# Gated mix of two linear-attention blocks: the load of B's wo moved behind the scratch round trip of M_A

## The chip, the cores and the metric

The kernel runs on one core of a Trainium2 chip. Times are device microseconds of one execution. The engines are PE (TensorE, matmuls; its weight loads are listed apart as PEld), DVE (VectorE), ACT (ScalarE), POOL (GpSimd) and SP (SyncE, which here only issues DMAs).

## The reference

Two linear-attention blocks A and B with their own weights read the same input x (2048 rows of 640, bf16; 32 heads of 20). Their outputs are mixed by a gate per row.

```python
def _A_ref(x, wqkv, wo):          # _B_ref is the same
    q, k, v = ...                 # (x @ wqkv), split into 32 heads of 20
    phi = lambda t: jnp.where(t > 0, t + 1, jnp.exp(t)) + 1e-6
    pq, pk = phi(q), phi(k)
    kv = jnp.einsum("bhsd,bhse->bhde", pk, v)
    z = jnp.einsum("bhsd->bhd", pk)
    num = jnp.einsum("bhqd,bhde->bhqe", pq, kv)
    den = jnp.einsum("bhqd,bhd->bhq", pq, z)[..., None] + 1e-6
    o = num / den
    return (heads of o side by side) @ wo

g = sigmoid((x * gate_w).sum(-1, keepdims=True))
return g * a + (1 - g) * b
```

## The kernel before

The kernel never forms v. It computes G = xᵀ·phi(k) (640 by 640), from it KV of each head by a product with wv and a mask, and M = KV·wo, one 640 by 640 matrix for each block. With the gate and the denominators folded into the scaled queries pqA and pqB, the output is pqA·M_A + pqB·M_B. Most large products are done by a Strassen-like scheme (sums of blocks on DVE, seven products in place of eight on PE, the products added up in PSUM).

The order of the work is written out by hand: within a `manual_schedule` block each engine runs its instructions in the order of the program, and waits on semaphores where it needs another's result. DMAs are issued by SP in program order too (the loads of the start and two of the last stores also by ACT). An instruction of SP that waits holds all that stand behind it.

The part around the change is the end of the third part, from the last k chunks of B to the first products of the output:

- `g_pass(1, DT - 1, 0, ...)` (L897; matmuls L424) makes the fifth block of rows of G of B in two runs of matmuls. Between the runs, and after it, six calls of `m_block` (L868) make M_A: each multiplies a masked block of 120 rows of KV of A (40 rows in the last) with `woA`, the wo of A (PE L872), and ACT copies the result into `M[0]` (the tile `MA`; the sixth into a tile `m`) at L877. SP then stores these rows into `m_rows`, a scratch tensor in DRAM (L878).
- `z_rows` (L510, PE L516) sums phi(k) of B over the rows, between the fourth and the fifth `m_block`.
- A DMA (L903) then reads all of `m_rows` back into `M[0]`. The rows come back in another order: row 5p + m goes to partition p, place m. It waits for all six stores to land.
- `p_diff` and `g_strassen(1, ...)` (L906; matmuls L453) follow: the other four fifths of G of B in seven products. Around the products, DVE does: `rec_pass` (L573, the reciprocals of the denominators), `k_sum(1, 4)`, then TM0, the difference of the two halves of M_A (L495, done by the helper at L592), which is the first reader of the reloaded `M[0]`; then `scale` (L642), five multiplications of pqB by R, the spread reciprocals, which ACT copies out of PSUM at L634; with two additions (L470, L508) that finish blocks of G. The addition of L470 reads a PSUM tile that a later product of PE adds to.
- After the stage, `kvt_mm` (L542, PE) and `kvt_mask` (L549, DVE) make KV of B, `p1` (L653) the first product of the output with `M[0]`, and `m_unit` and `m_half` (L567, PE) make M_B from KV of B and `woB`, the wo of B: the first readers of `woB`. From there to the end PE runs the products of the output (L653), DVE their additions (L658) and the sums of operands (L592), and SP stores the output (L673).

`load_wo(1, nc.sync)` (L735) loads `woB`, 800 KB, with one DMA issued by SP (L741). Its tile is the buffer of `woA` (one buffer in the pool `wpool` under the tag "wo"), so its DMA waits until the last matmul of the six `m_block`s has read `woA`. In the program it stands at L895, in front of the six stores of L878.

Of the kernel before, what the change touches and what calls it, by code (L numbers as in the profile page):

```python
# [32 lines left out]
def kernel(  # L33
# [11 lines left out]
    nc = tc.nc  # L45
# [12 lines left out]
    def new_stage(name):  # L58

        if stage:  # L60
            stage.pop().close()
        if name is not None:
            held = ctx.enter_context(ExitStack())
            stage.append(held)
            pools["ps"] = held.enter_context(late_pool(name))
# [373 lines left out]
    def k_sum(b, k):  # L439

        b11, b12 = [pk[:, 0:hc, n * HF:(n + 1) * HF] for n in range(2)]
        b21, b22 = [pk[:, hc:ST, n * HF:(n + 1) * HF] for n in range(2)]
        t = TK[b]
        left, right = {1: lambda: (b12, b11), 2: lambda: (b22, t[1]), 3: lambda: (b22, b12), 4: lambda: (b21, t[2])}[k]()
        add_rows(t[k], left, right, ALU.subtract)
# [148 lines left out]
    def p_diff(rows):  # L594

        up = slice(SH + rows.start, SH + rows.stop)
        add_rows(D3[:, :, rows], pqT[0][:, :, rows], pqT[0][:, :, up], ALU.subtract)
# [137 lines left out]
    def load_wo(b, eng):  # L735
        wo_sb[b] = wpool.tile([P, NG, D], BF16, tag="wo", name=f"wo{'AB'[b]}")
        if b == 0:
            eng.dma_start(out=wo_sb[0][:K6, 0:DT], in_=wo_dram[0][0:DT * K6].rearrange("(j p) f -> p j f", p=K6))
            eng.dma_start(out=wo_sb[0][:D - DT * K6, DT], in_=wo_dram[0][DT * K6:D])
            return  # L740
        eng.dma_start(out=wo_sb[b][:KG], in_=wo_dram[b].rearrange("(j p) f -> p j f", p=KG))  # L741
# [46 lines left out]
    with tc.manual_schedule():  # L788
# [79 lines left out]
        def m_block(g, slot):  # L868
            n = blocks[g][1]
            pt = ps("mA", slot)  # L870
            for hf in range(2):
                nc.tensor.matmul(  # L872
                    pt[:n, hf, 0:HF], lhsT=kv6[:n, g * K6:g * K6 + n], rhs=wo_sb[0][:n, g, hf * HF:(hf + 1) * HF],
                    start=True, stop=True,
                )
            to = M[0][:n, g, :] if g < DT else work.tile([P, D], BF16, tag="osb", name="m5", bufs=3)[:n]
            nc.scalar.copy(out=to.rearrange("p (b n) -> p b n", b=2), in_=pt[:n, :, 0:HF])  # L877
            nc.sync.dma_start(out=m_rows[g * K6:g * K6 + n, :], in_=to)  # L878
# [13 lines left out]
        TK[1][1] = t1[:]  # L892
        for k in (1, 2, 3):
            k_sum(1, k)
        load_wo(1, nc.sync)  # L895
        new_stage("after")
        g_pass(1, DT - 1, 0, lambda: [m_block(g, 2 + g) for g in (0, 1)])  # L897
        m_block(2, 2)
# [2 lines left out]
        m_block(4, 2)  # L901
        m_block(5, 3)
        nc.sync.dma_start(out=M[0][:], in_=m_rows[:].rearrange("(p m) d -> p m d", m=DT))  # L903
        part = [slice(n * RB, (n + 1) * RB) for n in range(4)]
        p_diff(part[0])
        g_strassen(1, lambda: z_pass(1, zr, 1), 3, 1)  # L906
# [105 lines left out]
```

## Time and profile before

| | us |
|---|---|
| median of 3 runs | 192.91 |
| lowest, highest run | 192.71, 193.56 |
| the profiled execution | 193.14 |
| its span | 191.4 |
| PE busy | 183.9 |
| DVE busy | 155.9 |
| ACT busy | 86.6 |
| POOL busy | 8.6 |

The profile is of one execution. Its span runs from the first to the last thing that it records; the execution's time holds a little more around it. A timeline row gives the start and the length in us, the engine and line, the operation with output and inputs, shapes, and how many instructions are merged; in brackets stands the idle time of the engine before it, and what ended it. "DMA to landing" is the time from the issue of a DMA by an engine to its last bytes. PE's ends are modelled: a row of matmuls that follow each other overlaps a little with the next, so starts are compared with starts. The granted clock of PE was 0.999 of full speed.

### The profile page before, as it was taken

The numbers are of one execution on the slowest core, as the hardware profiler recorded it, in microseconds if no ns is written. First come the engines' busy times: TensorE is split into PE (matmuls) and PEld (weight loads), VectorE is DVE, ScalarE is ACT, GpSimd is POOL, SyncE is SP. The second block draws the span as 40 slices with busy tenths as digits, with TensorE's granted clock in tenths as the row PEclk, the third lists the DMA queues.
The fourth block names the chain that finished last, engine by engine and source line by source line (L and its number), as shares of the span: only waits on it lengthen the run. The fifth ranks groups of instructions, "written<-read, shape, count | busy, mean of one in ns | idle before, by whom it ended". The sixth has DMA issues, their size and how long they took to land.

```text
span 191.4 us, 3678 instructions
## 1 busy us (share of the span) xinstructions
PE 183.9 (96%) x1485; PEld 123.7 (65%) x1494; DVE 155.9 (81%) x267; ACT 86.6 (45%) x134; POOL 8.6 (5%) x23
## 2 busy tenths in 40 slices
PE   8999999999999999999999999999968999999992
PEld 3666657765577677676666656766746776777771
DVE  1478868998998999997989878999397989788553
ACT  2055497555851622547786858642511611121110
POOL 8900000000000000000000000000000000000000
PEclk9999999999999999999999999999999999999999
DMA  6976449990050000005000000047400002312112
GB/s 192 305 146 69 99 82 323 328 251 32 2 171 3 0 0 0 3 0 171 0 3 2 0 0 3 0 122 224 171 0 3 0 3 87 118 41 103 69 69 70
DMA packets 19759, 15.64 MB, mean 82 GB/s; under 512 B 9502, under 2 KB 19614, under 8 KB 19742
## 3 DMA queue, kind: packets, MB, share of 16 engines
q1 hardware_dynamic: 18878, 14.59, 27.9%
q10 hardware_dynamic: 864, 0.82, 1.3%
q8 instruction: 11, 0.18, 0.4%
q14 instruction: 6, 0.05, 0.1%
HBM read 10.00 MB, written 3.44 MB: 70 GB/s over the span
## 4 chain that ended last, share of the span: by engine, by line
PE 84%; DVE 7%; DMA 5%; issue 1%; SPq 1%; ACT 1%; DVEq 0%; ACTq 0%
PE kA L250 12%; PE qA L294 11%; PE kB L250 11%; PE gs L453 9%; PE q L348 7%; PE ox L653 5%; PE oy L653 5%; PE oz L653 5%; DVE pqTB L642 3%; DMA m_rows<-m 3%; PE ow L653 2%; PE gB L424 2%; PE gA L424 2%; DMA MA<-m_rows 2%; PE warm L186 2%
## 5 line engine op out<-in xcount | busy, mean ns | idle before, releaser
L250 PEld LDWEIGHTS <-xT 128*128 128x128 bf16 x320 | 31.4, 99 | 15.0 <-issue 0.3
L230 DVE TENSOR_SCALAR e<-e 128x640 bf16<-128x640 bf16 (+2 forms) x56 | 19.3, 345 | 6.9 <-ACT e L225 6.7
L250 PE MATMUL kB<-wkB,xT 128*128 128x320 bf16 x160 | 24.2, 299 | 0.0
L250 PE MATMUL kA<-wkA,xT 128*128 128x320 bf16 x160 | 23.4, 306 | 0.0
L294 PE MATMUL qA<-xT,wqA 128*128 128x512 bf16 x96 | 22.2, 379 | 0.2
L294 PEld LDWEIGHTS <-wqA 128*128 128x128 bf16 x100 | 11.6, 118 | 9.3 <-issue 0.3
L225 ACT ACTIVATE e<-kA 128x640 bf16<-128x640 f32 x16 | 11.1, 704 | 12.4 <-PE kA L250 12.3
L453 PEld LDWEIGHTS <-xn 128*128 128x128 bf16 x128 | 12.2, 98 | 5.2 <-issue 0.5
L225 ACT ACTIVATE e<-kB 128x640 bf16<-128x640 f32 x16 | 11.3, 708 | 9.0 <-PE kB L250 8.9
L239 DVE SCALAR_TENSOR_TENSOR pk<-kA,e 128x640 bf16<-128x640 f32 x16 | 13.2, 825 | 1.7
L239 DVE SCALAR_TENSOR_TENSOR pk<-kB,e 128x640 bf16<-128x640 f32 x16 | 13.2, 824 | 1.5
L225 ACT ACTIVATE e<-qA 128x1024 bf16<-128x1024 f32 x10 | 10.2, 1023 | 8.6 <-PE qA L294 8.1
L697 ACT COPY u<-ox 128x320 f32<-128x320 f32 x8 | 3.4, 425 | 21.9 <-PE ox L653 21.9
L225 ACT ACTIVATE e<-q 128x512 bf16<-128x512 f32 x18 | 10.8, 597 | 5.4 <-PE q L348 3.8
L653 PEld LDWEIGHTS <-xT 128*128 128x128 bf16 x85 | 8.0, 98 | 3.1 <-DVE xT L592 0.2
L653 PEld LDWEIGHTS <-pqTA 128*128 128x128 bf16 x85 | 7.9, 98 | 2.9 <-issue 0.2
L653 PEld LDWEIGHTS <-pqTB 128*128 128x128 bf16 x80 | 7.8, 98 | 3.0
L453 PE MATMUL gs<-pk,xn 128*128 128x320 bf16 x64 | 9.5, 299 | 0.0
L348 PE MATMUL q<-xT,wqB 128*128 128x512 bf16 x32 | 9.5, 379 | 0.0
L658 DVE TENSOR_TENSOR osb<-oz,u 128x320 bf16<-128x320 f32 (+1 forms) x18 | 8.0, 452 | 1.6 <-PE oz L653 0.9
L681 ACT COPY p1s<-ox 128x320 f32<-128x320 f32 x8 | 3.4, 426 | 12.8 <-PE ox L653 12.8
L424 PEld LDWEIGHTS <-xn 128*128 128x128 bf16 x64 | 6.3, 98 | 3.0 <-issue 0.4
(145 smaller groups left out, 318.8 us busy)
## 6 DMA issues: line engine op xcount, KB each, us to landing
out_dram<-osb SPq DMA_DIRECT2D x14, 160.0 KB, 1.8
xn<-in_A_x_dram SPq DMA_DIRECT2D x3, 640.0 KB, 6.1
wqA<-in_A_wqkv_dram SPq DMA_DIRECT2D x1, 800.0 KB
wvA<-in_A_wqkv_dram SPq DMA_DIRECT2D x1, 800.0 KB, 9.3
wkB<-in_B_wqkv_dram SPq DMA_DIRECT2D x1, 800.0 KB, 6.1
wqB<-in_B_wqkv_dram SPq DMA_DIRECT2D x1, 800.0 KB
wvB<-in_B_wqkv_dram SPq DMA_DIRECT2D x1, 800.0 KB, 4.7
woB<-in_B_wo_dram SPq DMA_DIRECT2D x1, 800.0 KB, 6.3
```

The costliest lines, as they stand in the source:

```text
L186: nc.tensor.matmul(warm[:, 0, :], lhsT=one_l, rhs=one_r, start=True, stop=True)
L225: nc.scalar.activation(out=to, in_=part, func=ACT.Exp)
L230: nc.vector.tensor_scalar(self.e, self.e, 1.0, EPS, op0=ALU.min, op1=ALU.add)
L239: nc.vector.scalar_tensor_tensor(out=dst, in0=src, scalar=1.0 + EPS, in1=e, op0=ALU.add, op1=ALU.max)
L250: nc.tensor.matmul(pt[:, hf, 0:HF], lhsT=xT[:, c, i * P:(i + 1) * P], rhs=wk[b][:, c, hf * HF:(hf + 1) * HF], start=(c == 0), stop=(c == D ...
L294: nc.tensor.matmul(dst, lhsT=mixed(wq[b][:, c, :], m), rhs=xT[:, c, n * HB:(n + 1) * HB], start=first, stop=last,)
L348: nc.tensor.matmul(dst, lhsT=left(c), rhs=right(c), start=first and k == 0, stop=k == len(cs) - 1, skip_group_check=not first,)
L424: nc.tensor.matmul(pt[:, hf, 0:HF], lhsT=xn[:, i, c * P:(c + 1) * P], rhs=pk[:, i, hf * HF:(hf + 1) * HF], start=(i == 0), stop=(i == ST - 1),
L453: nc.tensor.matmul(pt[:, n, 0:HF], lhsT=left[:, i, n * P:(n + 1) * P], rhs=right[:, i, :], start=(first and i == 0), stop=(i == hc - 1), s ...
L642: nc.vector.tensor_tensor(out=pqT[b][:, m, :], in0=pqT[b][:, m, :], in1=rec, op=ALU.mult)
L653: nc.tensor.matmul(dst, lhsT=left[:, c, r0:r0 + P], rhs=right[:, c, :], start=(first and c == 0), stop=(c == DT - 1), skip_group_check=not ...
L658: nc.vector.tensor_tensor(out=dst, in0=acc, in1=sb, op=ALU.add)
```

## The change

The one call moves from its place in front of the stage "after" to a place behind the reload of `M[0]`. Everything else is the same text. After the change SP meets, in this order: six stores into `m_rows`, the reload of `M[0]` from it, the load of `woB`, the stores of the output.

```diff
         for k in (1, 2, 3):
             k_sum(1, k)
-        load_wo(1, nc.sync)
         new_stage("after")
         g_pass(1, DT - 1, 0, lambda: [m_block(g, 2 + g) for g in (0, 1)])
         m_block(2, 2)
@@ -901,6 +900,7 @@
         m_block(4, 2)
         m_block(5, 3)
         nc.sync.dma_start(out=M[0][:], in_=m_rows[:].rearrange("(p m) d -> p m d", m=DT))
+        load_wo(1, nc.sync)
         part = [slice(n * RB, (n + 1) * RB) for n in range(4)]
         p_diff(part[0])
         g_strassen(1, lambda: z_pass(1, zr, 1), 3, 1)
```

## The prediction

> **What bounds the kernel now.** The page first: its head, the busy times, and the shares of the chain that ended last.
>
> ```profile
> span 191.4 us, 3678 instructions
> PE 183.9 (96%) x1485; PEld 123.7 (65%) x1494; DVE 155.9 (81%) x267; ACT 86.6 (45%) x134; POOL 8.6 (5%) x23
> ...
> PE 84%; DVE 7%; DMA 5%; issue 1%; SPq 1%; ACT 1%; DVEq 0%; ACTq 0%
> ```
>
> PE is the bound: 191.4 - 183.9 = 7.5 us of the span is not PE's. But 7% of the chain is DVE and 5% DMA, so somewhere PE is held by them. The list of waits says where; columns are total us, times and longest:
>
> ```profile
> DVE TM L592 <- DMA MA<-m_rows: 3.3, 1, 3.3
> ...
> PE gs L453 <- DVE GT L470: 1.8, 1, 1.8
> ...
> PE mid L542 <- DVE KVT L549: 0.8, 1, 0.8
> ```
>
> These are one story. DVE idles 3.3 us for the reloaded M_A, and PE then waits twice (1.8 and 0.8) for DVE. A wait of SP's queue says why the reload was late (same columns), and the timeline of SP gives the times (start, us):
>
> ```profile
> SPq L741 <- PE mA L872: 39.4, 1, 39.4
> ```
>
> ```profile
> 125.17 0.34 SPq L741 DMA_DIRECT2D woB<-in_B_wo_dram  x1
> 125.61 2.71 SPq L878 DMA_DIRECT2D m_rows<-MA  x5
> 128.41 0.34 SPq L878 DMA_DIRECT2D m_rows<-m  x1
> ```
>
> SP issues in order. The load of wo of B (woB) takes woA's buffer, so it waits for the last matmul that reads woA; the six stores stand behind it and leave only from 125.61, although ACT had the first rows ready far earlier:
>
> ```profile
> 120.19 1.29 ACT L877 CAST MA<-mA 120x640 bf16<-120x640 f32 x2 [0.71 <-PE mA L872]
> ...
> 123.28 1.31 ACT L877 CAST MA<-mA 120x640 bf16<-120x640 f32 x2
> 124.80 0.69 ACT L877 CAST MA<-mA 120x640 bf16<-120x640 f32 x1 [0.21 <-PE mA L872]
> 125.39 0.68 ACT L877 CAST m<-mA 40x640 bf16<-40x640 f32 x1
> ```
>
> The landings, from the DMA issues of the page, from the view of line 878 and from the chain in order of time:
>
> ```profile
> woB<-in_B_wo_dram SPq DMA_DIRECT2D x1, 800.0 KB, 6.3
> ```
>
> ```profile
> DMA to landing us min/median/max: 5.7/5.9/6.1
> ```
>
> ```profile
> 128.41 5.13 DMA m_rows<-m
> 133.54 0.02 issue
> 133.56 4.29 DMA MA<-m_rows
> ```
>
> woB lands at 125.17 + 6.3 = 131.5. The first store, out at 125.61, took 5.7 us or more, so it landed not before 131.3; the last one at 133.54. The stores queue behind woB's bytes as well as behind its issue. The reload then lands at 133.56 + 4.29 = 137.85.
>
> **The change part by part.** Nothing is added or removed: one DMA issue of 0.34 us on SP moves behind six stores and one reload. The planned instruction order of PE, DVE, ACT and POOL stays as it was. There are four steps.
>
> (1) Stores. Freed of woB they leave behind their ACT copies: the first near 120.19 + 0.65 = 120.8, the fourth at 123.28 + 1.31 = 124.6, the fifth at 124.80 + 0.69 = 125.5, the last at 125.39 + 0.68 = 126.1 (126.2 with the issue of the fifth before it, 2.71 / 5 = 0.54 each). The last store thus leaves 128.41 - 126.2 = 2.2 us earlier.
>
> (2) Their landing. No row shows a store into the scratch with nothing ahead of it. The nearest are the stores of the output, also from 128 or fewer partitions into DRAM; the page's row and the spread over all 18 of them:
>
> ```profile
> out_dram<-osb SPq DMA_DIRECT2D x14, 160.0 KB, 1.8
> ```
>
> ```profile
> DMA to landing us min/median/max: 1.6/1.8/2.4
> ```
>
> Lower bound 1.6, upper bound 5.13 (the same store behind woB). I take 1.9, near the lower one: same direction, size and queue. Landing 128.1, against 133.54: 5.4 us earlier, of which 2.2 from the issue and 3.2 from the emptier queue.
>
> (3) The reload, issued at 128.1, with woB issued 0.4 us behind it. Alone it took 4.29, which gives 132.4. Worst, the two share the engines evenly and both end when both are done: woB and the 800 KB of stores together took 133.54 - 125.17 = 8.4 us, so 128.1 + 8.4 = 136.5. I take 132.4, since the stores behind woB landed after it, not beside it: a transfer of this queue waits for those ahead. The Trainium skill, "DMA: Bandwidth & Descriptors", section "Queues, rings and completion order", says that each DMA engine consumes descriptors in ring order but without a barrier between them; by the first half the reload keeps its 4.29, by the second it could lose some of it, and the landings here speak for the first half.
>
> (4) DVE and PE. DVE's timeline, with ACT's one row that matters:
>
> ```profile
> 133.88 1.94 ACT L634 CAST R<-exB 128x1024 bf16<-128x1024 f32 x2
> ```
>
> ```profile
> 133.18 1.43 DVE L592 TENSOR_TENSOR xT<-pk,xT 128x2560 bf16<-128x2560 bf16 x1
> 137.95 0.99 DVE L592 TENSOR_TENSOR TM<-MA 128x1600 bf16<-128x1600 bf16 x1 [3.34 <-DMA MA<-m_rows]
> 138.86 2.35 DVE L642 TENSOR_TENSOR pqTB<-pqTB,R 128x2048 bf16<-128x2048 bf16 x2
> 141.13 0.82 DVE L470 TENSOR_TENSOR GT<-gs,u 128x640 bf16<-128x640 f32 x1
> 141.86 3.49 DVE L642 TENSOR_TENSOR pqTB<-pqTB,R 128x2048 bf16<-128x2048 bf16 x3
> 145.26 0.88 DVE L508 TENSOR_TENSOR GT<-gs,u 128x320 bf16<-128x320 f32 x2
> 146.06 0.48 DVE L549 TENSOR_TENSOR KVT<-mid,maskE 80x320 bf16<-80x320 f32 x1
> ```
>
> DVE is free at 133.18 + 1.43 = 134.6. With M_A there at 132.4 it does TM0 (0.99) at once, until 135.6. The scaling then waits for R, which ACT ends at 133.88 + 1.94 = 135.82: start 135.87, not 138.86, so DVE's chain moves by 2.99. That is late next, and it caps the gain: landing before 134.9 buys DVE nothing more.
>
> PE in the same stretch:
>
> ```profile
> 135.72 2.34 PE L453 MATMUL gs<-T,S 128*128 128x320 bf16 x16
> 137.90 2.34 PE L453 MATMUL gs<-xT,xn 128*128 128x320 bf16 x16
> 142.00 2.33 PE L453 MATMUL gs<-pk,MB 128*128 128x320 bf16 x16 [1.76 <-DVE GT L470]
> 144.17 0.93 PE L542 MATMUL mid<-GT,wvB 128*80 128x80 bf16 x20
> 144.93 0.85 PE L653 MATMUL ox<-MA,pqTA 128*128 128x320 bf16 x5
> 146.59 0.93 PE L542 MATMUL mid<-GT,wvB 128*80 128x80 bf16 x20 [0.82 <-DVE KVT L549]
> ```
>
> A product follows the last after 137.90 - 135.72 = 2.18. So the product at 142.00 could start at 140.08. It needs the addition of L470, which with DVE 2.99 earlier ends at 141.13 + 0.82 - 2.99 = 138.96: no stall, 1.1 us to spare. The product ends at 140.08 + 2.33 = 142.41; the three scalings end at 141.86 + 3.49 - 2.99 = 142.36, so now the product, not DVE, releases L508, at 142.46. L508 to the mask to the second block of L542 took 146.59 - 145.26 = 1.33 in the trace, so that block starts at 143.79. PE alone, at 2.17 + 0.76 + 0.68 after 140.08, would come there at 143.69, so 0.10 of stall stays. Sum: 146.59 - 143.79 = **2.80 us** earlier (1.92 from the first stall, 0.88 from the second).
>
> Does that reach the end? The rest is PE's:
>
> ```profile
> 150.50:185.00 34.50, 34.50 (x269) 24.62 (x260) 27.46 (x60) 6.83 (x17) 0.00 (x0) 1.00 0.18 63
> ```
>
> Its columns are span, then busy time and instructions of PE, PEld, DVE, ACT and POOL, and the granted clock, DMA share and GB/s. PE has no gap there, DVE has 7 us spare, and what DVE does there hangs on PE's results, which all move together.
>
> woB itself is costed at nothing. Issued at 128.1 + 0.4 = 128.5 and behind the reload it lands near 132.4 + 6.3 = 138.7 at the latest (6.3 was with nothing ahead). Its first reader was at 148.12 and comes at 145.32 now:
>
> ```profile
> 148.12 0.34 PE L567 MATMUL mid<-woB,KVT 80*32 80x320 bf16 x4
> ```
>
> The cover is 6.6 us of PE and DVE work in front of L567; past it each us of delay costs one us. Behind woB on SP stand only the output stores, the first at 158.92 in the trace of before:
>
> ```profile
> 158.92 29.70 SPq L673 DMA_DIRECT2D out_dram<-osb  x16
> ```
>
> The profiled execution took 193.14 us, with 1.7 outside its span; 193.14 - 2.80 = 190.34, span 188.6. The median of the runs, 192.91, lies 0.23 lower, so 192.91 - 2.80 = **190.1 us** is the forecast.
>
> **The rivals.** (A) The reload shares with woB. It lands at 136.5; TM0 starts 0.1 later, 1.35 us earlier than before, and as DVE then sets the whole chain the gain is 1.35: 191.6. For it: one queue, 16 engines, 0.4 us apart. Against it: step 3's landings.
>
> (B) The stores' 5.1 us are their own, whatever is ahead. Then the last lands at 126.2 + 5.13 = 131.3, the reload at 135.6, and the gain is 137.85 - 135.6 = 2.2: 190.7. Against it: output stores of the same size land in 1.6 to 2.4.
>
> (C) No change: the reload comes early, but the time is given back, because DVE runs late in the outer stage once PE arrives there 2.8 us sooner: 192.9. For it: DVE is 81% busy. Against it: the last window, where DVE has slack and nothing is tied to a fixed time but woB.
>
> (D) Slower: woB becomes the late transfer. L567 waits for it; the gain shrinks from a landing at 145.3 on, is gone at 148.1, and the kernel is slower beyond. That takes 148.1 - 128.5 = 19.6 us from issue to landing; at 22 us the time would be 192.9 + 2.4 = 195.3. The longest landing among the page's DMA issues is that of woA:
>
> ```profile
> woA<-in_A_wo_dram SPq DMA_DIRECT2D x1, 750.0 KB, 13.5
> ```
>
> That would give 128.5 + 13.5 = 142.0, still in time. The same page of the Trainium skill, section "Rules for kernel authors", speaks against this change: issue a DMA early and wait for it late. By that rule woB's move gives up cover; in this trace it lands 16.6 us (148.12 - 131.5) before its use, and there is enough to give. That the change does not do what it says would need SP to hold the stores for something else, and their only live waits are ACT's copies.
>
> **How the numbers follow.** Forecast 0.75, A 0.09, B 0.06, C 0.06, D 0.04. The likeliest one's own range is 189.7 (192.71, the fastest run, less 2.9, the two stalls in full, and 0.1 of scatter) to 190.8 (fastest to slowest run is 0.85, mostly upward). B lies inside it; to take in A the range goes up to 191.7. Low 189.6, high 191.7, leaves C and D out and a little scatter. What a measurement of this kernel can tell from no change is 0.5%, 0.96 us. Faster by more: the forecast, A and B, 0.90, less 0.01 for an A at its worst; within: C and that, 0.07; slower: D, 0.04.
>
> **What would show it.** Step 1: the stores' issues at 120.9 to 126.2. Step 2: the reload's issue at 128.1 (131.3 is B). Step 3: TM0 no longer waits for the reload, which lands at 132.4 (136.5 is A). Step 4: TM0 at 134.6, scaling at 135.9, held by R; PE's 1.8 us wait gone and the 0.8 down to 0.1; L567 at 145.3 with no wait for woB. A wait of L567 on woB, a reload landing after 136.9, or a new PE gap after 150 would make the prediction wrong.

## The result and the profile after

| us | before | after |
|---|---|---|
| median of 6 runs | 193.28 | 190.77 |
| lowest, highest | 192.71, 194.54 | 190.44, 191.16 |
| the profiled execution | 193.14 | 191.16 |
| its span | 191.4 | 189.4 |

The ratio is 0.9862, with a 95% interval of 0.9826 to 0.9898: the kernel became faster, by 2.5 us of the medians. The forecast was 2.80 us.

The two profiled spans differ by 2.0 us only, less than the gain in the stage of the change. The reason lies at the start of the run, far from the change: the first matmul of gB (L424), which opens the stage, starts at 117.55 us before and at 118.42 after, 0.87 later, and 0.88 of it is there as early as the first matmul of L294 (11.74 and 12.62). So from here on a *stage time* is used: from the start of that first matmul to the start of the first matmul that reads `woB` (L567). Before, it is 148.12 - 117.55 = 30.57 us. PE's timeline after (start, us, engine and line, operation, idle time before it in brackets):

```profile
118.42 2.33 PE L424 MATMUL gB<-pk,xn 128*128 128x320 bf16 x16
...
136.58 2.34 PE L453 MATMUL gs<-T,S 128*128 128x320 bf16 x16
138.75 2.34 PE L453 MATMUL gs<-xT,xn 128*128 128x320 bf16 x16
140.93 2.34 PE L453 MATMUL gs<-pk,MB 128*128 128x320 bf16 x16
143.10 0.93 PE L542 MATMUL mid<-GT,wvB 128*80 128x80 bf16 x20
143.86 0.85 PE L653 MATMUL ox<-MA,pqTA 128*128 128x320 bf16 x5
144.64 0.92 PE L542 MATMUL mid<-GT,wvB 128*80 128x80 bf16 x20
...
146.17 1.29 PE L567 MATMUL mid<-woB,KVT 80*32 80x320 bf16 x32
```

The stage takes 146.17 - 118.42 = 27.75 us: 2.82 less. Neither of PE's two waits is there: no row of L453 or L542 has brackets, and the products follow each other at 2.17 to 2.18 us. The second block of L542 starts 144.64 - 143.86 = 0.78 after the first product of the output, whose five matmuls take 0.68; the 0.10 of stall is what the prediction left over. SP after the change:

```profile
121.78 4.92 SPq L878 DMA_DIRECT2D m_rows<-MA  x5
126.96 0.27 SPq L878 DMA_DIRECT2D m_rows<-m  x1
128.64 0.35 SPq L902 DMA_DIRECT2D MA<-m_rows  x1
129.08 0.38 SPq L741 DMA_DIRECT2D woB<-in_B_wo_dram  x1
```

The landings after, from the page's DMA issues (KB each, median us from issue to landing):

```profile
MA<-m_rows SPq DMA_DIRECT2D x1, 800.0 KB, 4.5
woB<-in_B_wo_dram SPq DMA_DIRECT2D x1, 800.0 KB, 7.7
...
m_rows<-MA SPq DMA_DIRECT2D x5, 150.0 KB, 2.0
```

The stores land 2.0 us after their issue, not 5.9. The reload goes out 10.22 us into the stage (128.64 - 118.42), before the change at 16.01, and takes 4.5. What DVE does with it:

```profile
134.04 1.43 DVE L592 TENSOR_TENSOR xT<-pk,xT 128x2560 bf16<-128x2560 bf16 x1
135.38 0.98 DVE L592 TENSOR_TENSOR TM<-MA 128x1600 bf16<-128x1600 bf16 x1
136.72 2.36 DVE L642 TENSOR_TENSOR pqTB<-pqTB,R 128x2048 bf16<-128x2048 bf16 x2 [0.35 <-ACT R L634]
139.03 0.82 DVE L470 TENSOR_TENSOR GT<-gs,u 128x640 bf16<-128x640 f32 x1
```

TM0 follows `k_sum` without a gap. The wait of 3.3 us for M_A is gone, and what holds DVE now is R, for 0.35 us.

### The profile page after: what moved, and what is told of

It is laid out like the page before. It is cut to its first block, busy times and chain, and to the rows that moved or that the text cites. A ratio compares the mean times of both kernels' runs of the same rounds, so it can differ in the third digit from the quotient of the medians.

```text
span 189.4 us, 3688 instructions
## 1 busy us (share of the span) xinstructions
PE 184.4 (97%) x1494; PEld 123.6 (65%) x1494; DVE 156.0 (82%) x267; ACT 86.7 (46%) x134; POOL 8.6 (5%) x23
## 4 chain that ended last, share of the span: by engine, by line
PE 91%; DMA 3%; DVE 2%; ACT 1%; ACTq 0%; issue 0%; DVEq 0%
PE gs L453 16%; PE qA L294 11%; PE kA L250 11%; PE kB L250 11%; PE q L348 7%; PE ox L653 6%; PE oy L653 5%; PE oz L653 5%; DMA xn<-in_A_x_dram 3%; PE ow L653 3%; PE gB L424 2%; PE gA L424 2%; PE qB L294 1%; PE q L294 1%; DVE osb L658 1%; PE mA L872 1%
## 5 line engine op out<-in xcount | busy, mean ns | idle before, releaser
L294 PE MATMUL qA<-xT,wqA 128*128 128x512 bf16 x100 | 22.4, 379 | 0.0
L294 PEld LDWEIGHTS <-wqA 128*128 128x128 bf16 x100 | 11.6, 118 | 9.3 <-issue 0.3
L453 PEld LDWEIGHTS <-xn 128*128 128x128 bf16 x128 | 12.2, 98 | 5.2 <-issue 0.5
L453 PE MATMUL gs<-pk,xn 128*128 128x320 bf16 x64 | 9.5, 299 | 0.0
L424 PEld LDWEIGHTS <-xn 128*128 128x128 bf16 x64 | 6.3, 98 | 3.0 <-issue 0.4
```

What stands on the lines that cost most here:

```text
L294: nc.tensor.matmul(dst, lhsT=mixed(wq[b][:, c, :], m), rhs=xT[:, c, n * HB:(n + 1) * HB], start=first, stop=last,)
L424: nc.tensor.matmul(pt[:, hf, 0:HF], lhsT=xn[:, i, c * P:(c + 1) * P], rhs=pk[:, i, hf * HF:(hf + 1) * HF], start=(i == 0), stop=(i == ST - 1),
L453: nc.tensor.matmul(pt[:, n, 0:HF], lhsT=left[:, i, n * P:(n + 1) * P], rhs=right[:, i, :], start=(first and i == 0), stop=(i == hc - 1), s ...
```

## The experiments

All times below are from the first matmul of gB, unless a row of a profile is shown. The landing of the reload is its issue and its length in the chain of waits, less that start. Each edit is shown against the changed kernel, that of the late TM0 against the kernel before.

**woB between the last store and the reload.** Half of the move: woB is no longer in front of the stores, but not yet behind the reload.

```diff
         m_block(5, 3)
+        load_wo(1, nc.sync)
         nc.sync.dma_start(out=M[0][:], in_=m_rows[:].rearrange("(p m) d -> p m d", m=DT))
-        load_wo(1, nc.sync)
```

> Stage time means: from the first matmul of gB (L424) to the first matmul that reads woB (L567); 30.57 us before, 27.75 after the change. All times here are from that first gB matmul. The theory: the stage takes 27.75 as long as the reload of M_A lands by 17.5 (135.05 - 117.55 in the trace of before), and each us later costs one us; before it landed at 20.3, after the change at 14.7. Here woB stands between the last store and the reload. The stores leave and land as after the change (the last at about 10.2). woB goes out at 8.9 and, alone on the queue behind them, lands near 13.6; the reload goes out at 10.2 behind woB's bytes and lands 2 to 3 us after them, at 16 to 17. Under 17.5: stage 27.75, the whole gain of 2.8 us. Rival, by which it is the place behind the reload that pays: the reload shares the engines with woB, lands near 18.5, stage 28.8, 1.0 us of the gain gone.

Measured: stage 28.24, 190.58 us, ratio 0.9836 (0.978 to 0.9891). The chain of this kernel:

```profile
125.79 1.64 DMA m_rows<-m
...
127.51 7.71 DMA MA<-m_rows
```

The 17.5 of the theory equals the reload's landing before, 20.30, less the 2.80 of the forecast. The stage began at 117.25, so the reload went out at 10.26 as after the change, and landed at 17.97: 0.47 past 17.5. The stage is 28.24 - 27.75 = 0.49 longer. Both theories missed their number; the rule with the threshold did not. What was mis-sized is woB's own transfer, 5.9 us here against the 4.7 put in for it; the reload came 3.2 us after it. So most of the gain lies in the stores, and a last half microsecond in the place behind the reload.

**woB in front of the last store alone.**

```diff
         m_block(4, 2)
+        load_wo(1, nc.sync)
         m_block(5, 3)
         nc.sync.dma_start(out=M[0][:], in_=m_rows[:].rearrange("(p m) d -> p m d", m=DT))
-        load_wo(1, nc.sync)
```

> woB stands between the fifth and the sixth store. SP holds nothing up: woB's last reader of woA ends at 7.6 (from the first gB matmul) and the sixth store leaves at about 8.5 as after the change. The theory, that a store also waits for the bytes ahead of it: woB lands at 13 to 14, the sixth store (50 KB) just behind it at 13.3 to 14.2, the reload goes out then and lands at 17.8 to 18.7, 0.3 to 1.2 past 17.5: stage 28.0 to 28.9. Rival, by which the old order cost only through SP standing still: sixth store landed at 10.5, reload near 16, stage 27.75.

Measured: stage 29.16, 191.14 us, ratio 0.9865 (0.9818 to 0.9912). SP's timeline and the chain:

```profile
120.74 4.92 SPq L878 DMA_DIRECT2D m_rows<-MA  x5
125.75 0.35 SPq L741 DMA_DIRECT2D woB<-in_B_wo_dram  x1
126.19 0.49 SPq L878 DMA_DIRECT2D m_rows<-m  x1
131.89 0.35 SPq L903 DMA_DIRECT2D MA<-m_rows  x1
```

```profile
126.19 5.68 DMA m_rows<-m
131.89 4.37 DMA MA<-m_rows
```

SP holds nothing back here: the sixth store leaves 126.19 - 117.37 = 8.82 into the stage, as after the change (8.54). Yet its 50 KB take 5.68 us to land, not 1.6, because woB's 800 KB are ahead. That is the share of the queue's bytes shown by itself. The reload lands at 14.52 + 4.37 = 18.89, 1.39 past the threshold, and the stage is 1.41 longer. The size expected was 0.3 to 1.2, again because woB took 5.9.

**One eighth of woB at the old place, the rest behind the reload.** SP stands still in front of the stores as before, with hardly any bytes ahead of them.

```diff
-        eng.dma_start(out=wo_sb[b][:KG], in_=wo_dram[b].rearrange("(j p) f -> p j f", p=KG))
+        rest_of_wo(eng, 0, 1)
+
+    def rest_of_wo(eng, lo, hi):
+        eng.dma_start(
+            out=wo_sb[1][:KG, lo:hi], in_=wo_dram[1][lo * KG:hi * KG].rearrange("(j p) f -> p j f", p=KG)
+        )
...
             k_sum(1, k)
+        load_wo(1, nc.sync)
         new_stage("after")
...
         nc.sync.dma_start(out=M[0][:], in_=m_rows[:].rearrange("(p m) d -> p m d", m=DT))
-        load_wo(1, nc.sync)
+        rest_of_wo(nc.sync, 1, NG)
```

> One eighth of woB (100 KB) is loaded at the old place, the other seven behind the reload. SP stands still in front of the stores as before, until woA is read at 7.6 (from the first gB matmul), but hardly any bytes are ahead of the stores. The theory: stores out from 7.8 to 10.2, the last landed about 12.2, reload landed at 16.5 to 16.9, under 17.5: stage 27.75 and the whole gain. Rival, by which the hold in SP's order was the cost: the stage stays near 30.6, or by the 2.2 us by which the last store leaves late, 29.9.

Measured: stage 27.76, 189.58 us, ratio 0.9781 (0.9732 to 0.9829). Its SP:

```profile
124.68 0.33 SPq L744 DMA_DIRECT2D woB<-in_B_wo_dram  x1
125.10 2.27 SPq L883 DMA_DIRECT2D m_rows<-MA  x5
127.47 0.31 SPq L883 DMA_DIRECT2D m_rows<-m  x1
129.31 0.35 SPq L908 DMA_DIRECT2D MA<-m_rows  x1
```

The last store leaves at 10.41, almost as late as before (10.86), but its way to the reload's issue takes 1.84 us, before 5.15. The whole stall is gone although the hold in SP's order is not: the reload goes out at 12.25 and takes 4.7, so it lands at 16.95, later than after the change, and still in time. So of the two halves of the old order the hold alone costs nothing, the bytes alone cost 1.4 us, and both together 2.8. (The bytes were tried with the last store alone behind them.)

**TM0 later, woB as before.** The other end of the chain: the transfers stay as late as they were, and their first reader on DVE moves into an idle stretch.

```diff
-        if b == 1:
-            add_rows(TM[0][:], M[0][:, :, HF:D], M[0][:, :, 0:HF], ALU.subtract)
...
             kvt_mask(kv, 0, 0)
+            add_rows(TM[0][:], M[0][:, :, HF:D], M[0][:, :, 0:HF], ALU.subtract)
             pairs[0].p1()
```

> woB as before, in front of the stores; only DVE's sum TM0, the first reader of the reloaded M_A, moves behind the first mask of KV (L549), where DVE idled 1.0 us for PE in both traces and where 0.99 us of work fits. The theory (the reload costs through DVE's order alone): the reload lands at 20.3 as before, the scaling starts when R is there, 18.3 from the first gB matmul, stage 27.75, the whole gain with no DMA moved. Rival (PE waits for the reload, or for the transfers, in another way): stage over 28.5, at most 30.57.

Measured: stage 27.75, 190.36 us, ratio 0.9822 (0.9772 to 0.9872). SP and DVE of this kernel:

```profile
128.01 0.35 SPq L876 DMA_DIRECT2D m_rows<-m  x1
133.22 0.35 SPq L901 DMA_DIRECT2D MA<-m_rows  x1
```

```profile
135.38 2.36 DVE L640 TENSOR_TENSOR pqTB<-pqTB,R 128x2048 bf16<-128x2048 bf16 x2 [1.25 <-ACT R L632]
...
142.77 0.48 DVE L547 TENSOR_TENSOR KVT<-mid,maskE 80x320 bf16<-80x320 f32 x1
143.17 0.98 DVE L590 TENSOR_TENSOR TM<-MA 128x1600 bf16<-128x1600 bf16 x1
144.26 0.49 DVE L547 TENSOR_TENSOR KVT<-mid,maskE 80x320 bf16<-80x320 f32 x1
```

The reload goes out at 16.14, as late as before, and the same 2.82 us are gained. The scaling starts at 18.30, held by R alone. So what PE lost was not a wait for the transfers themselves: the cost ran through one sum on DVE that stood in front of the scaling.

**The reload twice.** The second copy waits for the first; nothing reads the first.

```diff
-        nc.sync.dma_start(out=M[0][:], in_=m_rows[:].rearrange("(p m) d -> p m d", m=DT))
+        for _ in range(2):
+            nc.sync.dma_start(out=M[0][:], in_=m_rows[:].rearrange("(p m) d -> p m d", m=DT))
         load_wo(1, nc.sync)
```

> The changed kernel, but M_A is reloaded twice, the second copy waiting for the first (one copy more than needed), woB behind both. Tests the point from which the reload's landing costs. Times from the first gB matmul. The theory: the second copy lands at 14.7 + 4.4 = 19.1, 1.6 past 17.5: stage 29.3 to 29.4, 1.6 us over the changed kernel, 1.2 under before. Rival, by which R's wait or PE's own work would cover more than I worked out: stage 27.75. Rival, by which all delay of the reload costs, cap or not: 27.75 + 4.4 = 32.1.

Measured: stage 29.71, 191.28 us, ratio 0.987 (0.9799 to 0.9941). The second copy went out at 14.88 and took 4.57: landed at 19.45, 1.95 past 17.5, and the stage is 1.96 longer. So 4.7 us of delay (19.45 - 14.7) cost 2.0.

**woB from ACT's queue.** It is issued by ACT in the place of the changed kernel, which in ACT's order comes behind the copy of the sixth block.

```diff
-        load_wo(1, nc.sync)
+        load_wo(1, nc.scalar)
```

> The changed kernel, but woB is issued by ACT, behind its copy of the sixth block, so on another queue: it goes out at about 8.6 from the first gB matmul, beside the last stores and the reload instead of behind them. The theory: with two queues at work the engines share, the last store lands at 10.5 to 12 and the reload, sharing with what is left of woB, at 15.5 to 17.3; still under 17.5, stage 27.75. Rival: sharing is worse than that, reload past 17.5, stage 28 or more. ACT's issue of 0.35 us fits in the 1.6 us that it idles there.

Measured: stage 28.97, 191.98 us, ratio 0.9919 (0.9885 to 0.9953). ACT's issue of woB, and the chain:

```profile
125.60 0.34 ACTq L741 DMA_DIRECT2D woB<-in_B_wo_dram  x1
125.73 0.68 ACT L877 CAST m<-mA 40x640 bf16<-40x640 f32 x1
```

```profile
126.44 5.84 DMA m_rows<-m
132.30 4.29 DMA MA<-m_rows
```

woB leaves at 7.71, nearly a microsecond earlier than expected (ACT issues it before the copy in front of it has begun), and the last store, 0.84 us later on the other queue, takes 5.84 us: as long as behind woB on its own queue (5.68). The rival was right: the two queues did not share as the theory had it, and the small store waited as long as it does behind woB on its own queue. Why is not shown. The reload landed at 18.70, and the stage is 1.22 longer for 1.20 past the threshold.

The six kernels in which the reload's landing can be read, against 27.75 plus what it is past 17.5:

| kernel | reload landed | 27.75 + excess | stage measured |
|---|---|---|---|
| changed | 14.7 | 27.75 | 27.75 |
| woB between | 17.97 | 28.22 | 28.24 |
| woB from ACT | 18.70 | 28.95 | 28.97 |
| woB before the last store | 18.89 | 29.14 | 29.16 |
| reload twice | 19.45 | 29.70 | 29.71 |
| before | 20.30 | 30.55 | 30.57 |

The first row and the last fit by construction, since 27.75 and 17.5 come from these two kernels. The four rows between them test the rule, and each is within 0.02 us.

The rule also tells what sets the 17.5. R lets the scaling start at 18.30; where the reload is late, the scaling starts later, as in these rows of "woB between" and of "reload twice":

```profile
136.22 2.35 DVE L642 TENSOR_TENSOR pqTB<-pqTB,R 128x2048 bf16<-128x2048 bf16 x2
```

```profile
137.31 2.35 DVE L642 TENSOR_TENSOR pqTB<-pqTB,R 128x2048 bf16<-128x2048 bf16 x2
```

They stand at 18.97 and, with the stage of that kernel beginning at 116.86, at 20.45: 0.67 and 2.15 past R. The stages are 0.49 and 1.96 longer, and in the other kernels of the table the difference is 0.18 to 0.19 us too. So about 0.2 us of a late scaling is free. The scaling starts 1.00 after the reload's landing (17.97 and 18.97, 19.45 and 20.45), so R alone would put the limit at 17.3. The last 0.2 fits PE, whose last product of L453 ends at 140.93 + 2.33 = 143.26 after the change, 0.04 in front of L508:

```profile
143.30 0.89 DVE L508 TENSOR_TENSOR GT<-gs,u 128x320 bf16<-128x320 f32 x2
```

**woB four times, and three times.** Each copy waits for the one before: the same data, later. It tests the cover that the move spends.

```diff
-        eng.dma_start(out=wo_sb[b][:KG], in_=wo_dram[b].rearrange("(j p) f -> p j f", p=KG))
+        for _ in range(4):
+            eng.dma_start(out=wo_sb[b][:KG], in_=wo_dram[b].rearrange("(j p) f -> p j f", p=KG))
```

> The changed kernel, but woB is loaded four times, each copy waiting for the one before (three copies more than needed). Tests the cover of woB. Times from the first gB matmul. The theory: the first copy lands at 18.4 as after the change, the others 4.5 to 4.8 us apart, the last at 32 to 33; L567 was to start at 27.75 and now waits for it, one us for one us: stage 32 to 33, 4.3 to 5.2 us over the changed kernel, so some 2 us slower than before. Rival: less cover than thought, for woB's readers stand in front of other work or PE's clock falls in the gap: more than 5.5 us over the changed kernel. Other rival: the late load is absorbed by other work of PE: under 3 us over it.

Measured, four: stage 36.18, 202.80 us, ratio 1.0458 (1.0379 to 1.0536). The last copy landed at 36.1; the copies took 8.2, then 5.7 each. L567 waited 8.35 us for it, and that is not all: 36.18 - 27.75 = 8.4 in the stage, but 202.8 - 190.8 = 12.0 in the whole. PE's clock has the rest; the stretches below show span, then busy time and instructions of PE, PEld, DVE, ACT, POOL, the granted clock, DMA share and GB/s:

```profile
145.00:149.00 4.00, 0.24 (x2) 0.00 (x0) 1.64 (x3) 0.42 (x1) 0.00 (x0) 1.00 0.59 107
149.00:151.00 2.00, 0.00 (x0) 0.00 (x0) 0.00 (x0) 0.00 (x0) 0.00 (x0) 0.66 0.85 236
151.00:162.00 11.00, 8.41 (x92) 4.68 (x93) 4.81 (x17) 3.16 (x6) 0.00 (x0) 0.50 0.16 32
162.00:164.00 2.00, 2.00 (x12) 1.23 (x11) 0.32 (x2) 0.00 (x0) 0.00 (x0) 0.67 0.00 0
```

PE stopped at 145.24, the clock fell to half some 4.4 us later, and came back only in the last stretch, some 10 us after PE was at work again (0.66 and 0.67 are each 0.7 of 2 us at full and the rest at half). Three copies:

> As the kernel with four loads of woB, but three. There the copies landed 8.2, 5.75 and 5.73 us apart and L567 waited 8.35 us, and PE's clock then fell to half for about ten us. Here the last copy lands at 10.66 + 8.2 + 5.75 + 5.73 = 30.4 from the first gB matmul, L567 waits 2.6 us: stage 30.4. If the clock holds through a gap of 2.6 us, the time is 2.7 us over the changed kernel and about that of before; the rival, that any gap of some us costs the clock, gives 4 us or more on top.

Measured: stage 30.04, 196.26 us, ratio 1.0128 (1.009 to 1.0166), beside 190.13 for the changed kernel in the same set of runs: 6.1 more, of which the stage has 30.04 - 27.75 = 2.3. The wait and the clock:

```profile
PE mid L567 <- DMA woB<-in_B_wo_dram: 2.2, 1, 2.2
```

```profile
144.80:147.10 2.30, 0.08 (x5) 0.02 (x4) 1.47 (x2) 0.43 (x1) 0.00 (x0) 1.00 0.59 114
147.10:149.00 1.90, 1.90 (x40) 1.46 (x44) 0.33 (x1) 0.81 (x2) 0.00 (x0) 0.68 0.00 0
149.00:154.00 5.00, 5.00 (x56) 2.77 (x49) 3.58 (x12) 2.35 (x5) 0.00 (x0) 0.50 0.00 0
154.00:155.00 1.00, 1.00 (x7) 0.60 (x5) 1.00 (x6) 0.00 (x0) 0.00 (x0) 0.69 0.09 16
```

A gap of 2.2 us was enough: the clock fell about 0.7 us after PE had started again (0.68 is 0.7 of 1.9 us at full and the rest at half) and stayed at half until about 154.6. Seven microseconds at half speed cost about 3.4. All six runs show the loss, with mean clocks of 0.973 to 0.981. The rival was right.

**Is one of the cures better?** The medians of kernels with the same stage time differed, 190.77 for the changed kernel and 189.58 for the one with an eighth in front, in different sets of runs. Both ran once more side by side, with a third that has the change and the late TM0.

> The changed kernel once more, beside the next one, to tell whether the 1.2 us by which the medians of the two differ (190.77 and 189.58, from different sets of runs) is theirs. Both stages took 27.75 us, and the program in front of the stage is the same, so the theory says that the difference comes from the loads at the start (the first gB matmul started at 118.42 us in one profile and 117.06 in the other) and varies from run to run: medians within 0.7 us here. Rival: loading the first eighth early is worth a microsecond of its own, seen again here.

> As for the run before: within 0.7 us of it by the theory, 1 us or more under it by the rival; the stage 27.75 again.

> The changed kernel with TM0 moved behind the first mask of KV as well: two cures of the same stall. The theory: nothing is left to cure, since with either of them PE comes to the stage's end with 0.1 us of stall; stage 27.75, the time within 0.7 us of the changed kernel. Rival: TM0 out of the way of the scaling gains more, stage 27.5 or less.

Measured: the changed kernel 190.13 us, ratio 0.9817 (0.9781 to 0.9853); an eighth in front 189.57, ratio 0.9807 (0.9759 to 0.9855); change and late TM0 190.14, ratio 0.9822 (0.9783 to 0.986). All three stages took 27.76. The differences are within 0.7 us, the intervals lie over each other, and no version is shown to beat the changed kernel. What varies between the profiles is, first, the start: over all those used here the stage began between 116.86 and 118.42 us. In the changed kernel's first profile a part of it is a wait of PE in front of the transposes at the start, which the profile of before doesn't have:

```profile
PE xt L210 <- DMA xn<-in_A_x_dram: 0.5, 1, 0.5
```

This wait is not the whole of it, for the late TM0 and the second profile with an eighth in front have one of 0.5 us too and began the stage at 117.08 and 117.24. Why the start varies stays open. Second, the end: from L567 to the end of the span both profiles with an eighth in front take 42.8 us, and so does that of the reload twice, where the other kernels that load woB once take 43.2 to 43.3. The half microsecond lies behind the last addition of DVE. It is about the difference of the two medians taken side by side (190.13 and 189.57), where both stages began within 0.02 us of each other; its cause is not shown either.

A buffer of its own for woB, which would take the wait for woA away without moving anything, was not tried.

## Why the prediction was right

Step 1, the stores, was right to 0.1 us: the last one was to leave 126.2 - 117.55 = 8.65 into the stage and left at 8.54.

Step 2, the landing, was a choice between 1.6 and 5.13. The last store took 1.6 to 1.7, the others 2.0; the value taken was 1.9. The reload went out at 10.22, expected at 10.55. Rival B, that 5.1 us are the store's own, is refuted by this alone; the kernel with woB in front of the last store shows the same 50 KB at 5.68.

Step 3, the reload, was taken at 4.29 and took 4.5 with woB 0.44 us behind it. Rival A would have had it land at 18.95 (136.5 - 117.55); it landed at 14.7. woB paid: 7.7 us, not 6.3.

Step 4 was right in every link: TM0 at once, the scaling at 18.30 (expected 135.87 - 117.55 = 18.32) and held by R, no stall of L453, 0.10 left in front of L542, 2.82 us of the stage against 2.80. That the gain has a cap, and where it lies, is shown by the four kernels of the table that test the rule, each within 0.02 us of it. Step 4 had put the cap at a landing at 134.9, 17.35 into the stage, with R as its cause; it lies at 17.5, and the last 0.2 us fit the product, which the same step named as what then releases L508. That the cost ran through TM0 is shown by moving TM0 alone.

Rival C, that the time is given back later, did not come: from L567 to the end of the span the profile took 191.4 - 148.1 = 43.3 us before and 189.4 - 146.2 = 43.2 after.

Rival D did not come either, with woB landed at 18.4 and read at 27.75: 9.4 us of cover left, against the 6.6 that the prediction had worked out as the least. But its price was wrong. The prediction charged a late woB one us for each us; the runs with three and four copies show 2.3 us more of the stage with 3.4 on top of it, and 8.4 with 4.5 on top (from L567 to the end of the span, 193.7 - 147.1 = 46.6 and 201.3 - 153.6 = 47.7, where the changed kernel takes 43.2). The break-even of D therefore lies not at 148.1 on the clock of before but earlier: three copies, landed at 30.0 into the stage, where one for one the kernel would still have been 0.5 under before, were 1.28% slower than it.

The time itself: 190.1 was forecast, 190.77 measured in one set of runs and 190.13 in another. By the ratio the gain is 2.0 to 3.4 us, and the stage says 2.82. In the two profiles the difference is the start of the run (2.82 less 0.87 is 1.95, beside the 2.0 of the spans). That the 2.5 us of the medians fall short of 2.82 for the same reason is likely, but not shown.

## What to carry to other kernels

A large load that waits for a buffer at the head of an in-order queue can delay what stands behind it in two ways: it holds their issues, and its bytes stand ahead of theirs. Before valuing a fix, find the point up to which the late transfer costs nothing (here 17.5 us, where R and PE's last product come next): delay within it is free, beyond it each us counts, and a delay that is free by itself can still add to another (here the hold cost nothing alone, the bytes 1.4 us, both 2.8). Where a transfer's first reader stands in the order of a busy engine, moving the reader can be as good as moving the transfer (here both gave a stage of 27.75), and cover for a load that the matmuls need should be counted with the clock in mind.

## What the runs showed of the hardware

Two microseconds of idle PE can cost more than themselves. The gaps of 1.76 and 0.82 us in the profile of before left the granted clock at 1.00 there; a gap of 2.2 us was followed by about seven us at half clock, and one of 8.35 us by about ten after PE had started again. The clock fell 2.9 us after PE had stopped in the first case (147.8 - 144.9) and 4.4 us in the second, so these two give no fixed delay. Nor is it shown that the gaps of the kernel before are always harmless: of its 31 runs beside the experiments five had a mean clock of 0.991 and took 193.91 to 195.28 us, while no listed run of the changed kernel is under 0.997. Those five have no trace. The Trainium skill, "TensorE: Matmul & The Clock Gate", section "Why this matters for your kernels", asks for no idle gap over some 3 us. Here less than that was enough. What PE ran around the gap were short matmuls, some of them on part of the array (L542 in front of it, L567 behind it); whether that is why the clock took the gap as longer was not tried.

A second queue did not protect a small store from a large load: the 50 KB took 5.84 us to land with woB just ahead on ACT's queue, 5.68 with it ahead on SP's own, and 1.6 to 1.7 with woB behind them.
